# A gated linear recurrence with a gated feed-forward layer: two units transposed by DMA instead of on TensorE, float32 running sums in four units, four gate blocks in a bank, eighteen unread groups of products, and a new order of work

## The chip, the cores and the metric

The kernel runs on one core of a Trainium2 chip. The metric is the device time of one execution in microseconds. A core has five engines, each with its own in-order stream of instructions: TensorE (PE in the profile; its weight loads are PEld), VectorE (DVE), ScalarE (ACT), GpSimd (POOL) and SyncE (SP). Sixteen DMA engines move the data; here SP issues the loads, the stores and the DMA transposes, and POOL issues the weight loads and some small copies inside the core.

## The reference

Four batches of eight heads, 768 positions, head size 48. A complex decay per position and channel, its magnitude capped at 0.999, drives a linear recurrence; its real part gives the attention output, which is reshaped to 3072 rows of 384 and passed through a gated feed-forward layer of 1536 columns.

```python
mag = np.sqrt(a_re * a_re + a_im * a_im)
scale = np.minimum(mag, 0.999) / (mag + 1e-06)
a_re_n, a_im_n = (a_re * scale, a_im * scale)
for t in range(S):
    new_re = ar * S_re - ai * S_im          # ar, ai: a_re_n, a_im_n at t
    new_im = ar * S_im + ai * S_re
    kv = np.einsum('bhd,bhe->bhde', k[:, :, t], v[:, :, t])
    S_re, S_im = (new_re + kv, new_im)
    y[:, :, t] = np.einsum('bhd,bhde->bhe', q[:, :, t], S_re)
# x: y as 3072 x 384
g = x @ w_gate
gelu = 0.5 * g * (1.0 + erf(g * inv_sqrt2))
val = x @ w_val
ffn_out = gelu * val @ w_out
res_gate = 1.0 / (1.0 + np.exp(-(x @ w_res)))
return (x + res_gate * ffn_out)
```

## The kernel before

The 768 positions of a batch are cut into six chunks of 128, so there are 24 tiles (batch, chunk). They are handled in 14 units: units 0 and 1 hold the first chunk of batches 0 and 1, unit 2 the first chunk of batches 2 and 3, units 3 to 11 two tiles each (two batches of the same chunk), and units 12 and 13 the last chunk of batches 2 and 3.

A unit goes through three functions.

- `prepare` loads a_re, a_im, q, k and v of its tiles (192 KB a load, L373). ACT takes the logarithm of a_re (L394), its inverse by an exponential (L395), and, with the ratio a_im / a_re made at L397, the logarithm of the magnitude (L399, L402, L403) and the angle (L433). Both are summed along the 128 positions by a product with a triangular matrix. The summand is first split into a rounded part and a rest in the type fp32r (lh and ll, L406 and L408, for the logarithm; th and tl, L334 and L452, for the angle), and `sums` (L355, products at L359) adds two products for each tile. The capped sums are turned into exponentials (L423, L424), the angles are reduced to one turn (L462, L464) and turned into sines and cosines (L477). The last row of the angles is carried into the next chunk of the same batch by a small DMA with addition (L439, L445). From these, queries and keys with real and imaginary parts are made (L482, L487) and transposed: in units 0 to 7 on TensorE (L504, eight transposes a tile and side, followed by a copy of 96x1024 out of PSUM), from unit 8 on by a DMA transpose that SP issues (L496). `PE_T = 8` sets that.
- `attend` makes the masked products of queries and keys (L535, L538), the attention output (L547, L549) and the carried state (L559 to L572).
- `forward` transposes x (L591 on TensorE for units 0 to 2, L583 by DMA afterwards) and runs the gates and values: 12 blocks of 128 columns, two blocks to a PSUM bank, each with three products (L605). GELU on ACT (L610) and a product on DVE (L611) follow each bank. In a unit of two tiles a bank of two blocks is 512 columns wide, in a unit of one tile 256. Then come the residual gate (L620, L622), the output in three steps of four products a tile (L631), and the last two products and sums (L635, L638) before the store (L640).

Every function adds steps to a plan. The order of the 1450 steps is a list of numbers written out by hand or by a tool, `ORDER`, and the engine of many steps is written in `PLACE`. `Plan.run` walks the list; each engine gets its steps in that order, buffers and PSUM banks are handed out along it (25 wide buffers, eight banks), and a table of ACT functions is loaded (L652) whenever the next step needs another of the three sets. Some kinds of DVE and POOL steps (`PORT`) are made to wait for each other in turn. The weights come in POOL's stream (L340): six loads each for the gate and value weights (wg, wv), one for the residual weights (wr), three for the output weights (wo).

Of the kernel before, what the change touches and what calls it, by code (L numbers as in the profile page):

```python
# [9 lines left out]
FP = mybir.dt.float32  # L10
# [10 lines left out]
PE_T = 8  # L21
SL, ST = 1,1
WD = 25
# [7 lines left out]
    24: "DVE", 33: "DVE", 40: "DVE", 50: "DVE", 51: "ACT", 53: "ACT", 64: "ACT", 104: "POOL", 114: "ACT", 116: "POOL",  # L31
    132: "ACT", 145: "ACT", 190: "DVE", 191: "DVE", 203: "DVE", 213: "DVE", 223: "DVE", 225: "ACT", 236: "DVE", 252: "ACT",
    305: "DVE", 306: "DVE", 318: "DVE", 322: "ACT", 323: "POOL", 330: "DVE", 340: "DVE", 345: "DVE", 347: "ACT", 353: "DVE",
    422: "DVE", 435: "DVE", 438: "POOL", 446: "DVE", 460: "DVE", 463: "ACT", 551: "DVE", 554: "POOL", 555: "POOL", 562: "DVE",
    572: "DVE", 576: "DVE", 585: "DVE", 595: "DVE", 667: "DVE", 670: "ACT", 671: "POOL", 686: "ACT", 688: "DVE", 692: "DVE",
    771: "DVE", 786: "POOL", 787: "POOL", 821: "DVE", 866: "DVE", 872: "DVE", 899: "DVE", 902: "POOL", 903: "POOL", 910: "DVE",
    933: "DVE", 984: "DVE", 1014: "ACT", 1015: "POOL", 1050: "DVE", 1088: "DVE", 1121: "ACT", 1124: "POOL", 1125: "POOL",
    1151: "DVE", 1160: "DVE", 1198: "DVE", 1232: "POOL", 1233: "POOL", 1240: "DVE", 1251: "ACT", 1257: "DVE", 1304: "DVE",
    1325: "POOL", 1329: "DVE", 1344: "DVE", 1376: "DVE", 1396: "ACT", 1397: "POOL", 1410: "ACT", 1448: "DVE",
}  # L40
ORDER = [
    97, 98, 16, 102, 293, 17, 103, 410, 104, 21, 105, 22, 106, 294, 23, 24, 411, 179, 115, 295, 34, 35, 116, 296, 117, 107, 25,
    178, 118, 303, 26, 36, 420, 27, 37, 108, 119, 28, 100, 181, 180, 413, 304, 109, 120, 421, 110, 305, 121, 38, 29, 188, 30,
    111, 39, 306, 412, 307, 32, 99, 182, 189, 308, 112, 309, 190, 31, 125, 191, 319, 310, 101, 526, 41, 321, 122, 40, 19, 18,
    123, 320, 42, 113, 183, 299, 204, 422, 124, 205, 127, 130, 33, 527, 423, 436, 206, 43, 207, 528, 20, 529, 184, 44, 126, 314,
    192, 46, 128, 316, 193, 210, 45, 322, 208, 424, 194, 47, 195, 49, 211, 323, 131, 129, 199, 52, 196, 209, 48, 536, 315, 311,
    212, 324, 135, 425, 50, 537, 1, 185, 298, 137, 437, 54, 200, 132, 114, 138, 538, 312, 136, 198, 325, 313, 326, 426, 55, 327,
    300, 759, 297, 186, 758, 53, 7, 141, 56, 133, 197, 539, 139, 328, 643, 642, 213, 134, 201, 214, 51, 329, 60, 438, 140, 57,
    216, 439, 58, 144, 202, 2, 187, 330, 215, 334, 12, 552, 217, 8, 332, 553, 6, 0, 219, 331, 218, 226, 336, 142, 220, 768, 333,
    143, 222, 227, 145, 224, 62, 440, 761, 645, 644, 301, 302, 225, 335, 441, 223, 769, 554, 221, 242, 343, 443, 59, 555, 61,  # L50
    339, 243, 63, 240, 652, 64, 344, 444, 341, 233, 231, 442, 241, 228, 234, 317, 244, 445, 653, 146, 760, 337, 5, 342, 232,
    559, 540, 340, 874, 4, 654, 3, 245, 150, 235, 154, 560, 338, 556, 875, 561, 236, 85, 170, 360, 87, 152, 350, 156, 166, 203,
    345, 148, 361, 81, 354, 65, 171, 9, 10, 168, 446, 11, 83, 229, 162, 427, 73, 13, 164, 158, 77, 67, 75, 351, 417, 416, 160,
    557, 89, 355, 541, 79, 90, 69, 358, 74, 431, 558, 230, 71, 151, 318, 359, 770, 251, 364, 348, 365, 66, 155, 153, 349, 433,
    428, 432, 68, 362, 429, 14, 76, 363, 771, 430, 163, 655, 346, 82, 86, 70, 147, 84, 78, 347, 157, 656, 149, 249, 72, 165,
    167, 252, 159, 237, 172, 250, 884, 367, 15, 238, 357, 257, 91, 885, 88, 169, 269, 352, 80, 562, 542, 784, 447, 657, 92, 415,
    253, 239, 161, 448, 261, 543, 414, 273, 173, 366, 93, 353, 563, 564, 668, 877, 369, 174, 658, 450, 876, 434, 669, 254, 94,
    175, 368, 452, 263, 255, 449, 258, 265, 277, 259, 455, 986, 419, 418, 278, 451, 459, 267, 533, 988, 279, 256, 886, 785, 457,
    456, 275, 453, 458, 274, 280, 454, 1206, 370, 670, 435, 659, 372, 464, 374, 386, 460, 271, 671, 246, 465, 530, 382, 887,
    276, 260, 248, 1097, 388, 376, 390, 466, 461, 467, 384, 474, 476, 480, 544, 95, 1207, 392, 247, 531, 356, 475, 786, 547,  # L60
    270, 371, 468, 545, 532, 477, 548, 549, 787, 272, 469, 675, 1096, 772, 373, 262, 266, 281, 481, 987, 773, 546, 1216, 672,
    660, 534, 646, 989, 484, 535, 176, 676, 264, 268, 888, 550, 677, 478, 470, 788, 471, 479, 791, 566, 889, 663, 462, 662, 661,
    792, 96, 673, 282, 793, 287, 1106, 674, 375, 996, 568, 565, 288, 283, 463, 789, 665, 997, 485, 387, 567, 1107, 664, 647,
    473, 284, 177, 289, 391, 571, 575, 573, 377, 389, 285, 790, 900, 396, 394, 649, 648, 577, 290, 551, 678, 1098, 393, 486,
    998, 679, 572, 569, 286, 574, 680, 510, 570, 506, 487, 378, 764, 291, 576, 901, 681, 1208, 592, 650, 488, 774, 490, 511,
    397, 775, 1099, 502, 380, 492, 383, 590, 482, 683, 504, 498, 508, 591, 385, 593, 881, 651, 1306, 1209, 902, 582, 491, 999,
    395, 500, 903, 689, 379, 489, 586, 685, 381, 493, 483, 690, 1000, 594, 398, 583, 1108, 686, 776, 779, 907, 765, 595, 778,
    580, 587, 399, 581, 781, 780, 908, 1217, 596, 794, 601, 400, 904, 578, 682, 584, 472, 777, 880, 292, 1378, 684, 404, 905,
    597, 499, 1109, 579, 585, 909, 600, 1218, 687, 1311, 503, 688, 628, 691, 405, 762, 401, 763, 599, 666, 906, 1122, 696, 890,
    507, 692, 706, 795, 402, 698, 406, 505, 697, 501, 403, 693, 512, 699, 1379, 878, 1012, 589, 520, 610, 509, 1219, 796, 911,  # L70
    708, 494, 407, 1013, 618, 707, 408, 602, 709, 879, 614, 782, 598, 798, 513, 612, 629, 620, 992, 995, 1123, 604, 496, 1307,
    616, 495, 710, 700, 603, 766, 797, 891, 895, 767, 892, 619, 896, 799, 497, 1001, 521, 701, 893, 1383, 910, 716, 615, 800,
    1384, 711, 617, 1385, 1312, 894, 897, 605, 522, 783, 913, 1014, 514, 801, 611, 802, 810, 805, 898, 1313, 515, 806, 882, 717,
    1124, 523, 702, 607, 703, 621, 712, 516, 1015, 912, 1230, 613, 803, 606, 726, 804, 517, 1215, 899, 1002, 914, 993, 883, 994,
    990, 622, 1003, 608, 807, 728, 667, 588, 734, 811, 915, 808, 738, 730, 722, 991, 917, 736, 723, 916, 732, 624, 609, 814,
    623, 824, 713, 918, 740, 724, 815, 812, 822, 1314, 1016, 1004, 1213, 625, 813, 725, 825, 1220, 1006, 1019, 823, 1007, 727,
    694, 731, 524, 518, 1125, 809, 1033, 695, 1020, 1315, 729, 816, 1017, 525, 920, 919, 1021, 636, 817, 1018, 704, 1009, 1008,
    1005, 1316, 735, 1025, 519, 1102, 828, 718, 626, 637, 705, 720, 733, 737, 714, 926, 638, 1231, 1386, 832, 826, 1022, 639,
    719, 818, 630, 1026, 827, 627, 1308, 1210, 833, 1100, 927, 640, 715, 829, 1322, 721, 1129, 631, 1024, 936, 1126, 924, 937,
    641, 921, 632, 1394, 925, 1127, 739, 1232, 1130, 819, 633, 1381, 1023, 928, 1128, 929, 1028, 744, 752, 746, 934, 742, 747,  # L80
    753, 842, 1027, 1221, 1131, 1387, 1110, 741, 409, 831, 935, 1031, 1032, 1323, 1395, 844, 1309, 1030, 846, 754, 1132, 938,
    1222, 944, 939, 1317, 1111, 1112, 848, 743, 1223, 858, 834, 847, 1103, 836, 1113, 945, 745, 859, 1045, 838, 748, 930, 755,
    634, 835, 840, 1029, 1046, 849, 1324, 1114, 1047, 922, 830, 1212, 1048, 1133, 843, 1117, 1233, 1211, 1101, 635, 923, 931,
    1134, 837, 839, 1224, 950, 845, 1325, 1105, 1310, 749, 1038, 850, 1318, 1119, 1116, 1118, 841, 1319, 1115, 1136, 1104, 1320,
    1036, 1039, 946, 851, 966, 756, 1321, 1225, 1037, 1226, 1049, 757, 1135, 1380, 854, 972, 1050, 821, 852, 1214, 948, 853,
# [101 lines left out]
def kernel(  # L187
# [25 lines left out]
    if SPLIT:  # L213
        units[-SPLIT:] = [[x] for u in units[-SPLIT:] for x in u]
    NU = len(units)
    where = {bc: (p, i) for p, u in enumerate(units) for i, bc in enumerate(u)}
    size = [len(u) for u in units]

    ctx.enter_context(tc.manual_schedule())
# [463 lines left out]
```

## Time and profile before

| | us |
|---|---|
| median of the three runs shown | 262.35 |
| lowest and highest run | 261.4, 591.57 |
| the profiled execution | 262.78 |
| its span, first to last instruction | 261.0 |

The profile is one execution. It gives each engine's busy time (TensorE 226.4 us, DVE 225.4, ACT 214.1, POOL 94.5), the same by stages, the groups of instructions by line and form with the mean duration and what ended the idle time ahead of them, the waits, and a chain of work followed back from the last instruction. Of that chain TensorE has 71%, DMA 11%, ACT 9%. Over the span, HBM was read with 31.26 MB and written with 4.72 MB. "Clock" is the TensorE clock that the throttle granted, as a share of full speed; its mean was 0.978.

### The profile page before, as it was taken

To read this page: it belongs to the slowest core of one execution; us is meant where nothing else is said; L and a number is where in the kernel's file an instruction comes from. 1 tells how busy PE (TensorE), PEld (TensorE's weight loads), DVE (VectorE), ACT (ScalarE), POOL (GpSimd) and SP (SyncE) were. 2 spreads that over 40 slices of the span, in tenths; PEclk is the share of its full clock that TensorE was granted. 3 is DMA by queue.
4 is the path that set the end of the run, shared out by engine and by line. 5 is a ranking of instruction groups with operands and counts; after the bars stand their busy time and mean duration, and the time that the engine had idled before them with its cause. 6 is when DMAs were issued, how large, how long until landed. Compare 5 with 4: busy or idle time off the path is not lost.

```text
span 261.0 us, 6358 instructions
## 1 busy us (share of the span) xinstructions
PE 226.4 (87%) x2426; PEld 181.8 (70%) x2426; DVE 225.4 (86%) x404; ACT 214.1 (82%) x355; POOL 94.5 (36%) x114
## 2 busy tenths in 40 slices
PE   0230992889999999999999999999999999999993
PEld 0120772778978977877878877778778777887881
DVE  2589889999899999999999999999999794965363
ACT  4999999899899999999998999999988684241240
POOL 3013086196605743576625634351420001110110
PEclk9999996599999999999999999999999999999998
DMA  8999999989999997995989896999757919402111
GB/s 141 187 187 186 187 194 192 213 163 213 202 184 172 167 186 163 221 146 124 211 149 190 148 179 149 182 168 236 133 114 160 117 23 136 133 3 63 60 63 60
DMA packets 162174, 39.83 MB, mean 153 GB/s; under 512 B 155617, under 2 KB 162145, under 8 KB 162145
## 3 DMA queue, kind: packets, MB, share of 16 engines
q1 hardware_dynamic: 157696, 35.53, 79.4%
q0 software_dynamic: 4448, 3.90, 9.3%
q8 instruction: 19, 0.31, 0.5%
q14 instruction: 11, 0.08, 0.1%
HBM read 31.26 MB, written 4.72 MB: 138 GB/s over the span
## 4 chain that ended last, share of the span: by engine, by line
PE 71%; DMA 11%; ACT 9%; DVE 3%; POOL 2%; SPq 1%; issue 1%; POOLq 0%; DVEq 0%
PE pb L605 32%; PE pb L631 17%; PE pb L359 6%; PE pb L620 4%; PE pb L504 4%; PE pb L535 3%; DMA wo<-in_moe_w_out_dram 3%; DMA wv<-in_moe_w_val_dram 2%; DMA ai<-in_a_im_dram 2%; ACT L652 2%; DMA t<-fr 2%; DMA ar<-in_a_re_dram 2%; POOL t L397 1%; PE pb L549 1%; PE pb L547 1%; ACT CS L477 1%
## 5 line engine op out<-in xcount | busy, mean ns | idle before, releaser
L610 ACT ACTIVATE h<-pb 128x512 bf16<-128x512 f32 (+1 forms) x84 | 41.2, 547 | 23.2 <-PE pb L631 13.0
L605 PE MATMUL pb<-xT,wv 128*128 128x256 bf16 (+1 forms) x504 | 58.1, 257 | 0.4 <-DMA wv<-in_moe_w_val_dram 0.4
L605 PE MATMUL pb<-xT,wg 128*128 128x256 bf16 (+1 forms) x504 | 57.0, 257 | 0.0
L631 PE MATMUL pb<-wo,h 128*128 128x384 bf16 x288 | 56.5, 326 | 0.0
L611 DVE SCALAR_TENSOR_TENSOR h<-h,pb 128x512 bf16<-128x512 bf16 (+1 forms) x84 | 48.5, 602 | 4.2 <-PE pb L605 2.8
L605 PEld LDWEIGHTS <-wg 128*128 128x128 bf16 x504 | 42.9, 98 | 7.1 <-issue 0.8
L652 ACT ACT_TABLE_LOAD x36 | 46.2, 1283 | 1.3 <-PEq L667 0.7
L605 PEld LDWEIGHTS <-wv 128*128 128x128 bf16 x504 | 41.9, 98 | 7.5 <-issue 1.3
L638 POOL TENSOR_TENSOR ot<-ot,x 128x384 f32<-128x384 f32 x16 | 14.6, 913 | 65.0 <-DVE Gb L567 23.4
L631 PEld LDWEIGHTS <-h 128*128 128x128 bf16 x288 | 26.3, 97 | 13.0 <-issue 0.4
L538 DVE TENSOR_TENSOR am<-pb,mask 128x512 bf16<-128x512 f32 x48 | 31.9, 680 | 2.9 <-PE pb L535 2.8
L397 POOL TENSOR_TENSOR t<-t,ai 128x768 f32<-128x768 f32 (+1 forms) x10 | 16.0, 1601 | 18.1 <-DVE fK L487 9.0
L504 PE MATMUL pb<-ident,fK 128*128 128x128 bf16 x112 | 10.0, 246 | 13.5 <-DVE fK L487 13.5
L359 PE MATMUL pb<-th,ut_one 128*128 128x384 f32 x24 | 11.3, 471 | 11.4 <-POOL th L334 11.1
L452 POOL TENSOR_TENSOR tl<-t,th 128x768 fp32r<-128x768 f32 (+1 forms) x10 | 16.5, 1656 | 10.4 <-DVE ll L408 7.8
L635 DVE SCALAR_TENSOR_TENSOR ot<-sg,pb 128x384 f32<-128x384 f32 x24 | 13.1, 547 | 6.8 <-PE pb L631 5.0
L504 PEld LDWEIGHTS <-fK 128*128 128x128 bf16 x112 | 8.4, 112 | 15.0 <-DVE fK L487 14.3
L535 PE MATMUL pb<-QT,KT 96*128 96x128 bf16 x192 | 17.7, 225 | 0.5 <-DMA QT<-fQ 0.4
L535 PEld LDWEIGHTS <-KT 96*128 96x128 bf16 x192 | 13.8, 101 | 3.9 <-issue 2.2
L622 ACT ACTIVATE sg<-pb 128x384 f32<-128x384 f32 x24 | 11.6, 502 | 5.3 <-PE pb L620 2.8
L620 PE MATMUL pb<-wr,xT 128*128 128x384 bf16 x72 | 15.5, 326 | 0.0
L423 ACT ACTIVATE E<-pb 128x384 f32<-128x384 f32 x24 | 11.5, 500 | 3.2 <-PE pb L359 3.0
(91 smaller groups left out, 472.2 us busy)
## 6 DMA issues: line engine op xcount, KB each, us to landing
ar<-in_a_re_dram SPq DMA_DIRECT2D x24, 192.0 KB, 4.6
ai<-in_a_im_dram SPq DMA_DIRECT2D x24, 192.0 KB, 4.6
k<-in_k_dram SPq DMA_DIRECT2D x24, 192.0 KB, 4.4
q<-in_q_dram SPq DMA_DIRECT2D x24, 192.0 KB, 4.5
vf<-in_v_dram SPq DMA_DIRECT2D x24, 192.0 KB, 4.3
out_dram<-ot SPq DMA_DIRECT2D x24, 192.0 KB, 2.8
wg<-in_moe_w_gate_dram POOLq DMA_DIRECT2D x6, 192.0 KB, 5.6
wv<-in_moe_w_val_dram POOLq DMA_DIRECT2D x6, 192.0 KB, 5.9
```

Of the source, the lines that this page charges most:

```text
L359: nc.tensor.matmul(out=bank.tile, lhsT=ut_one, rhs=x[:, i * DM:(i + 1) * DM], start=(j == 0), stop=(j == 1))
L397: add(e1, "tai", lambda: on[e1].tensor_tensor(out=F("t"), in0=F("t"), in1=flat(T("ai"), n), op=OP.mult), [s["ai"]], [s["t"]], n)
L452: add(e10, "tl", lambda: on[e10].tensor_tensor(out=F("tl"), in0=F("t"), in1=F("th").bitcast(FP), op=OP.subtract), [s["t"], s["th"]], [s["t ...
L504: nc.tensor.transpose(out=tp.tile[:, h, :], in_=s[g].tile[:, i * H + h], identity=ident)
L535: nc.tensor.matmul(out=ap.tile[:, h, :], lhsT=kT.tile[0:DD, u * H // 2 + h, :], rhs=qT.tile[0:DD, u * H // 2 + h, :], start=True, stop=True)
L538: add("DVE", "am", lambda u=u, am=am, ap=ap: nc.vector.tensor_tensor(out=am.tile[:, u * H // 2:(u + 1) * H // 2, :], in0=ap.tile, in1=mask ...
L605: nc.tensor.matmul(out=o_.tile[:, u, :], lhsT=w_[:, k_, (2 * m + u) * 128:(2 * m + u + 1) * 128], rhs=s["xT"].tile[:, k_, 0:n].rearrange(" ...
L610: add("ACT", "gelu", lambda gp=gp, hv=hv: nc.scalar.activation(out=hv(), in_=gp.tile, func=AF.Gelu), [gp], [hh], n, "G")
L611: add("DVE", "h", lambda vp=vp, hv=hv: nc.vector.scalar_tensor_tensor(out=hv(), in0=hv(), scalar=0.5, in1=vp.tile, op0=OP.mult, op1=OP.mul ...
L620: nc.tensor.matmul(out=rp.tile, lhsT=s["xT"].tile[:, k_, i, :], rhs=wr[:, k_, :], start=(k_ == 0), stop=(k_ == KF - 1))
L631: nc.tensor.matmul(out=op_.tile, lhsT=s["h2"].tile[:, k_, i * 128:(i + 1) * 128], rhs=wo[:, k_, :], start=(k_ == 0), stop=(k_ == NF - 1))
L652: plan.run(ORDER, lambda table: nc.scalar.preload_act_table_set(ACT_SETS[table]), after)
```

## The change

The constants, and with them what is done in which unit:

```diff
-PE_T = 8
-SL, ST = 1,1
-WD = 25
+PE_T = 6
+PF_L, PF_T = 4, 4
+WD, WQ = 25, 5
+CSB = 2
+QUAD = 14
+WARM = 18
...
-PLACE = { (the old engines)
+PLACE = { (new engines for many steps)
...
-ORDER = [ (1450 steps)
+ORDER = [ (1400 steps)
```

`PE_T = 6`: units 6 and 7 are transposed by DMA too. `PF_L = PF_T = 4`: units 0 to 3 sum in float32, with one product for each sum and no split; the cap is applied in place (`cap`) and lh, ll, th and tl are not made. `QUAD = 14` leaves every unit in a group of its own, so the new functions for groups (`prepare` cut into `logs`, `angles`, `features`) work on one unit at a time, as before. a_re is loaded straight into the buffer of its logarithm.

```diff
-            if SL:
+            if p >= PF_L:
                 add("PE", "cumL", lambda i=i: sums(clm[i], i, F("lh"), F("ll")), [s["lh"], s["ll"]], [clm[i]])
             else:
...
+                add("PE", "cumL4", lambda i=i: nc.tensor.matmul(out=clm[i].make([128, DM]), lhsT=ut_f, rhs=P("la", p)[:, i],
+                                                               start=True, stop=True), [V["la"][p]], [clm[i]])
...
-        if ST:
+        if p >= PF_T:
             e9 = place("DVE")
...
+                add("PE", "cumT4", lambda i=i: nc.tensor.matmul(out=cth[i].make([128, DM]), lhsT=ut_f, rhs=P("t", p)[:, i],
+                                                               start=True, stop=True), [V["t"][p]], [cth[i]])
```

In `forward` a bank holds `w` blocks, two in a unit of two tiles and four in a unit of one:

```diff
-        for m in range(NF // 2):
+        w = 512 // (n * 128)
+        for m in range(NF // w):
...
-                    o_.make([128, 2, n * 128])
-                    for u in range(2):
+                    o_.make([128, w, n * 128])
+                    for u in range(w):
...
-            hv = lambda m=m: s["h2"].tile[:, 2 * m:2 * m + 2, 0:n * 128]
+            hv = lambda m=m: s["h2"].tile[:, w * m:w * m + w, 0:n * 128]
```

Eighteen groups of eight products of the identity with itself are added, each into a bank that nobody reads, and placed by the list:

```diff
+    for _ in range(WARM):
+        wb = Bank()
+
+        def f(wb=wb):
+            wb.make([128, 512])
+            for _ in range(8):
+                nc.tensor.matmul(out=wb.tile[:, 0:128], lhsT=ident, rhs=ident, start=True, stop=True)
+        add("PE", "warm", f, (), [wb])
```

The product that updates the carried state (`Gb`) may now be placed on POOL, and is in 11 of its 16 steps. Steps by kind, where they differ (old and new): gate and value steps 168 and 144, GELU 84 and 72, transposes of queries and keys on TensorE 28 groups and 20, by DMA 20 and 28, table loads of ACT 36 and 30. Of the 18 unread groups 14 stand ahead of the first gate step in the new list.

## The prediction

> **What bounds the kernel now.** I read the busy time by stages first, then the chain that ended last, then the groups by form, then the transfer queue's waits. The stages (length, busy time with counts, granted TensorE clock, DMA share, GB/s):
>
> ```profile
> core 0: us, PE busy (x) PEld busy (x) DVE busy (x) ACT busy (x) POOL busy (x), PEclk, DMA share, GB/s
> 0.00:55.40 55.40, 26.13 (x198) 19.85 (x198) 43.74 (x78) 49.72 (x79) 20.25 (x34) 0.91 1.26 183
> 55.40:256.70 201.30, 200.25 (x2236) 161.93 (x2231) 180.50 (x325) 164.38 (x278) 74.26 (x81) 1.00 0.81 145
> 256.70:261.00 4.30, 0.00 (x0) 0.00 (x0) 1.11 (x2) 0.00 (x0) 0.00 (x0) 0.84 0.24 91
> ...
> 45.00:51.50 6.50, 4.59 (x35) 3.90 (x36) 6.40 (x9) 5.25 (x7) 1.40 (x3) 0.50 1.21 209
> ```
>
> The first gate product starts at 55.42. Before it TensorE works 26.1 of 55.4 us while ACT works 43.4 of the 45.4 us from 10 to 55.4: ACT's queue, with DVE, sets when the gates begin. From there TensorE idles 1.05 us in 201.3, then comes a tail of 4.3. So the time is start + TensorE's work behind it + tail. The chain (start, length, what) gives the two waits behind the start, and TensorE's pace:
>
> ```profile
> 58.50 5.66 DMA wv<-in_moe_w_val_dram
> 64.21 0.51 PE pb L605 x6
> ...
> 70.11 7.25 DMA wo<-in_moe_w_out_dram
> ...
> 97.87 0.66 PE pb L605 x6
> 98.52 1.30 PE pb L631 x8
> ...
> 101.78 1.34 PE pb L504 x24
> 103.12 0.97 PE pb L620 x6
> ...
> 131.53 0.69 PE pb L359 x4
> ```
>
> A gate or value step of six products costs 0.655 us, an output step of four 0.65, a residual step 0.49, eight transposes 0.45, one running sum (a pair in fp32r) 0.345. Four query-key products cost 0.223 (0.22 to 0.23 in the same view).
>
> **The parts.** Rows used (line, form, count | busy, mean ns | idle before):
>
> ```profile
> L652 ACT ACT_TABLE_LOAD x36 | 46.2, 1283 | 1.3 <-PEq L667 0.7
> L408 DVE SCALAR_TENSOR_TENSOR ll<-la,lh 128x768 fp32r<-128x768 f32 x10 | 9.4, 949 | 0.1
> L610 ACT ACTIVATE h<-pb 128x256 bf16<-128x256 f32 x24 | 7.9, 396 | 11.8 <-PE pb L631 9.5 <-PE pb L605 2.3
> L521 PE MATMUL pb<-idf,mr 16*96 16x16 f32 x18 | 3.0, 242 | 0.0
> ```
>
> *TensorE's work behind the first gate product.* I count the steps that each list places behind it. Alike in both: gates and values 94.5 us, output 46.8, residual 11.8, query-key 8.9, the rest of attention and its small steps about 14.8; 176.8 together. The old list adds 17 transpose groups (7.7) and 34 running sums (11.5): 196.0, for which the chip took 201.3, a share of 0.973. The new list adds 10 groups (4.5), 30 sums (10.2) and 4 of the unread groups (8 x 0.056 = 0.45 each, the pace of 128-column gates at 248.13: 54 in 3.02 us), less one small step of 0.2: 193.1. At the same share: 198.4. **-2.9 us.**
>
> *The start.* ACT must run 70 instructions and 7 table loads before the old first gate, 74 and 7 before the new one: by mean durations 55.4 and 56.5 us. ACT's instructions overlap (241.7 us of durations make 214.1 busy, 0.886): **+1.0 us**. The loads needed first rise from 40 to 41, inside the same microsecond.
>
> *Float32 sums in units 0 to 3.* These drop ll, th and tl of four units (0.36 to 1.8 us each on DVE, POOL or ACT) and run 12 products in float32 in place of 12 pairs. No row shows a float32 product of 384 columns. Nearest below: the pair, 0.345. Above: the widest fp32r rows, 0.69 each early on, twice: 1.38 against a cold pair at 0.64. So 0 to +8.9 us of TensorE, in a stage where it idles 29.3. I take nothing on the end, since ACT sets the start; ends: -2.0 (ACT's idle time from 10 to 55.4, all of it) to +8.9. L521, already float32, shows 22 rows for 11 products. [...]
>
> *Unread groups.* 14 of the 18 stand ahead of the first gate, 6.3 us at full pace and 12.6 at half, where TensorE idles 29.3: nothing. What they can give: at clock 0.50 (45 to 51.5) four transpose groups came 0.87 us apart where 0.45 is the later pace, 1.7 us. I take 0, because ACT and POOL (a cast ends at 55.16, just ahead of the last attention product before the gate) are as late; ends -1.7 and 0.
>
> *Units 6 and 7 by DMA.* The eight groups are counted above; their eight copies (1.01 on ACT, 0.68 on DVE) lay beside TensorE. Added: eight issues on SP of 1.29 us, landing after 3.5, each waiting for its product tile with loads queued behind it. I take 0, as the list leaves units 8 and 9 their loads 4 us or more ahead of use; the other end is the second rival.
>
> *Four blocks a bank.* In the four single-tile units ACT goes from 24 x 0.396 to 12 x 0.607 us (-2.2), DVE from 24 x 0.414 to 12 x 0.677 (-1.8); TensorE streams the same columns. Beside TensorE: 0; in the tail the last value block's pair, 0.6 + 0.7 us, lies under three output steps and one residual step, 2.4 us.
>
> *The list.* Table loads fall from 36 to 30, 7.7 us of ACT, none ahead of the first gate. ACT idles 36.9 us behind the start, so 0; at most TensorE's last 1.05 idle goes. The weights: the last wv load moves from place 297 to 290 with its first use at 312 to 341, the last wo from 373 to 352. Their waits (0.43 and 0.28 us) stay inside the share of 0.973.
>
> **Sum.** The profiled execution took 262.78 us (span 261.0). 262.78 - 2.9 + 1.0 = 260.9; it lay 0.43 above the median of the runs, 262.35, so **260.4 us**.
>
> **Rivals.**
>
> 1. *Faster: the start comes early.* If the warm clock gives its 1.7 us, ACT loses its idle 2.0 and TensorE its 1.05: 260.4 - 4.75 = 255.7. For it: ahead of the new gate ACT has done ten roundings and sixteen exponentials of sums against seven and twelve, so less preparation is left behind it. Against: DMA is at 183 GB/s over the whole stage, and the same bytes must come. [...] Chance 0.30.
>
> 2. *Slower: SP becomes the bound.* Its waits, one of them shown (waiter, released by: us in all, times, longest):
>
> ```profile
> SPq L496 <- DVE am L538: 9.6, 3, 7.3
> ```
>
> With the other rows of L496 they add to 25.2 us for 20 transposes, 1.26 each; with the issue, 2.55. Eight more in the stretch from 84 to 142, where SP has gaps of 6.5 us in all, delay what stands behind by 20.4 - 6.5 = 13.9. The queries of unit 8 were issued by 127.5 and read at 136.2; less 4.5 for landing, 4.2 of slack. So DVE, and TensorE behind it, come 9.7 late: **270.1**. It decides once SP's added time there passes 10.7. For it: the waits are long when the list has a transpose early. Against: in that stretch many loads hold SP 1.0 to 2.4 us where 0.4 is the least, so part of the queue is DMA time that goes on during a wait. Chance 0.17.
>
> 3. *The float32 products hold the start.* One fp32r product over 384 columns took 0.32 us at half clock (starts at 34.56, 34.88, 35.20), a pair 0.64. If a float32 product takes two pairs, near the upper end above, twelve add 7.7; nine unread groups at half pace add 8.1. Together they pass the 13.2 us that TensorE idles from 10 to 40 by 2.6, at worst by all 7.7. Middle: +5.2, 265.6. For it: L521's two rows for each product. [...] Against: these products come early in each unit, when ACT has other units' work queued. Chance 0.08.
>
> That the unread products are dropped is no rival: all 144 stand in TensorE's program.
>
> **How the numbers follow.** Forecast 0.45, rivals 0.30, 0.17 and 0.08. The forecast's own range takes in -3.7 (1.7 + 2.0) and +5.2: 256.7 to 265.6. The range that should hold 8 in 10 reaches to rival 1 with the share of 0.973 gone too (-5, at 251) and to rival 2 (270). Two per cent, about what a measurement of this kernel can tell from no change, are 257.1 and 267.6. Faster: 0.27 of rival 1 and 0.04 of the forecast, 0.31. Slower: rival 2 and 0.02 of rival 3, 0.19. Within: 0.50.
>
> **What would show it.** First gate product near 56.4; span from there to TensorE's last product near 198.4; 30 table loads; transposes by TensorE 160 in place of 224. Clock under 1.00 from 40 to 51 would say the unread groups do not keep it. A float32 sum near 0.65 us or twice that, and ACT idle with TensorE as releaser before 50, would speak for rival 3; L496 waits of over 10 us from 100 to 140, with DVE waiting for q or k, for rival 2. Wrong altogether: a start before 52, or TensorE idle for more than 5 us behind it.

## The result and the profile after

The changed kernel is a little slower, where a little faster was forecast.

| | before | after |
|---|---|---|
| median of 20 runs, us | 262.18 | 263.49 |
| profiled execution, us (span) | 262.78 (261.0) | 263.42 (261.4) |
| start of the first gate product, us | 55.42 | 57.48 |
| from there to TensorE's last product, us | 201.3 | 199.9 |
| of it TensorE idle, us | 1.05 | 2.89 |
| tail, us | 4.30 | 4.04 |

Ratio after to before: 1.0057, 95% interval 1.0034 to 1.0079. The difference is below the two per cent that the prediction names, but clear of zero, and its sign is not the forecast's.

The busy time by stages of the changed kernel (length, busy time with counts, granted clock, DMA share, GB/s), to be read against the same stages of before:

```profile
core 0: us, PE busy (x) PEld busy (x) DVE busy (x) ACT busy (x) POOL busy (x), PEclk, DMA share, GB/s
0.00:57.46 57.46, 35.33 (x312) 25.56 (x313) 41.99 (x75) 51.62 (x83) 20.87 (x38) 0.91 1.20 186
57.46:257.36 199.90, 197.01 (x2201) 158.79 (x2197) 174.09 (x295) 151.94 (x257) 66.89 (x76) 1.00 0.88 154
257.36:261.40 4.04, 0.00 (x0) 0.00 (x0) 1.11 (x2) 0.00 (x0) 0.00 (x0) 1.00 0.26 97
45.00:51.50 6.50, 5.19 (x71) 4.50 (x69) 6.47 (x11) 6.16 (x10) 3.88 (x5) 0.90 1.24 192
```

Behind the start TensorE is busy 197.0 us in place of 200.25, so the saving of 3.2 us is there. It is more than given back by a start 2.06 us later and by 1.84 us more idle time. TensorE's waits from 55.4 us on (who waited for whom: us, times, longest):

```profile
PE pb L621 <- DVE am L612: 1.1, 1, 1.1
PE pb L609 <- DMA QT<-fQ: 0.8, 1, 0.8
PE pb L681 <- DMA xT<-x: 0.6, 1, 0.6
PE pb L681 <- DVE h L687: 0.5, 1, 0.5
PE pb L609 <- DVE KT L362: 0.5, 1, 0.5
PE pb L633 <- DVE fK L561: 0.4, 1, 0.4
```

The first stands just ahead of the first gate product, the others are the new idle time; the wait for QT (at 127.46) is for the second tile of unit 6, one of the two units moved to DMA transposes. The chain that ended last (start, length, what) no longer shows the weights, as it did before (wv at 58.50, wo at 70.11), but ACT, a carry by DMA and DVE until 71 us, and TensorE from there on:

```profile
53.84 0.75 ACT t L441
54.97 1.82 POOL t L444
56.81 0.84 ACT s L447
...
66.19 3.52 DMA t<-fr
69.83 0.86 DVE th L362
70.69 0.60 DVE h L687
71.33 1.50 PE pb L681 x24
```

Where the saving went shows when both kernels are compared at one moment, 85 us, a point taken behind the loads of all weights. The transfers of both kernels up to there, before first:

```profile
DMA packets 66622, 15.83 MB, mean 186 GB/s; under 512 B 63158, under 2 KB 66614, under 8 KB 66614
```

```profile
DMA packets 65561, 15.65 MB, mean 184 GB/s; under 512 B 62096, under 2 KB 65552, under 8 KB 65552
```

And the groups of TensorE behind 85 us, by form, of before and then of after:

```profile
L605 PE MATMUL pb<-xT,wv 128*128 128x256 bf16 x342 | 45.9, 273 | 0.0
L605 PE MATMUL pb<-xT,wg 128*128 128x256 bf16 x318 | 41.1, 273 | 0.0
...
L504 PE MATMUL pb<-ident,fQ 128*128 128x128 bf16 x48 | 3.7, 219 | 0.0
L504 PE MATMUL pb<-ident,fK 128*128 128x128 bf16 x48 | 3.5, 219 | 0.0
```

```profile
L681 PE MATMUL pb<-xT,wv 128*128 128x256 bf16 x360 | 46.7, 273 | 0.0
L681 PE MATMUL pb<-xT,wg 128*128 128x256 bf16 x343 | 43.5, 273 | 0.6 <-DMA xT<-x 0.6
...
L578 PE MATMUL pb<-ident,fK 128*128 128x128 bf16 x16 | 1.2, 220 | 0.0
```

Both kernels have moved nearly the same bytes by then (0.18 MB apart). The new one has 80 transposes fewer left (96 and 16; 80 x 0.056 = 4.5 us) but 43 gate and value products of 256 columns more (660 and 703; 43 x 0.109 = 4.7 us). The stages on both sides of 85 us, with the columns of the first table, two lines of before and then two of after:

```profile
55.42:85.00 29.58, 28.92 (x390) 24.38 (x387) 28.07 (x56) 27.97 (x51) 15.83 (x18) 1.00 1.18 192
85.00:256.70 171.70, 171.31 (x1849) 137.53 (x1846) 152.42 (x270) 136.38 (x228) 58.40 (x63) 1.00 0.74 137
```

```profile
57.48:85.00 27.52, 26.09 (x400) 22.64 (x396) 26.60 (x46) 26.44 (x41) 14.44 (x17) 1.00 1.13 180
85.00:257.36 172.36, 170.90 (x1803) 136.13 (x1801) 147.47 (x250) 125.48 (x217) 52.44 (x60) 1.00 0.84 150
```

Behind 85 us TensorE's work is nearly equal, 171.3 and 170.9 us. That the new kernel has more gate work left is decided ahead of 85 us: from the first gate product to there TensorE worked 28.9 us before and 26.1 after, for the start is 2.06 later and the idle time 0.8 longer, and 1.35 of the 26.1 went to three unread groups: 4.2 us less. In the same stretch the new kernel did 24 transposes more (64 against 40, 1.3 us) and six residual products fewer (1.0 us), which makes it 4.5.

### The profile page after: what moved, and what is told of

Read it like the earlier page. It is cut to its first block, busy times and chain, and to the rows that moved or that the text cites. A ratio compares the mean times of both kernels' runs of the same rounds, so it can differ in the third digit from the quotient of the medians.

```text
span 261.4 us, 6476 instructions
## 1 busy us (share of the span) xinstructions
PE 232.3 (89%) x2506; PEld 184.4 (71%) x2506; DVE 217.2 (83%) x371; ACT 203.6 (78%) x339; POOL 87.8 (34%) x113
## 4 chain that ended last, share of the span: by engine, by line
PE 63%; ACT 15%; DMA 9%; issue 4%; DVE 4%; POOL 2%; SPq 1%; DVEq 0%; POOLq 0%; ACTq 0%
PE pb L681 30%; PE pb L707 16%; PE pb L387 4%; PE pb L696 4%; PE pb L609 3%; ACT L737 3%; DMA t<-fr 2%; DMA xT<-x 2%; DMA ai<-in_a_im_dram 2%; DMA QT<-fQ 2%; POOL t L444 2%; DMA la<-in_a_re_dram 2%; ACT t L453 2%; ACT CS L463 2%; PE pb L623 1%
## 5 line engine op out<-in xcount | busy, mean ns | idle before, releaser
L686 ACT ACTIVATE h<-pb 128x512 bf16<-128x512 f32 x72 | 40.2, 604 | 22.0 <-PE pb L681 21.3
L681 PE MATMUL pb<-xT,wv 128*128 128x256 bf16 (+1 forms) x504 | 56.4, 257 | 0.5 <-DVE h L687 0.5
L687 DVE SCALAR_TENSOR_TENSOR h<-h,pb 128x512 bf16<-128x512 bf16 x72 | 47.4, 678 | 10.8 <-PE pb L681 8.8
L681 PE MATMUL pb<-xT,wg 128*128 128x256 bf16 (+1 forms) x504 | 55.1, 257 | 0.6 <-DMA xT<-x 0.6
L642 POOL TENSOR_TENSOR Gb<-U,M 96x384 bf16<-96x384 f32 x11 | 9.3, 873 | 22.1 <-DVE fK L561 11.2
L475 DVE SCALAR_TENSOR_TENSOR la<-s,la 128x768 f32<-128x768 f32 (+1 forms) x14 | 11.7, 838 | 5.8 <-ACT s L450 5.2
L529 POOL TENSOR_TENSOR tl<-t,th 128x768 fp32r<-128x768 f32 (+1 forms) x8 | 12.9, 1608 | 9.8 <-DVE fQ L561 3.3
L444 POOL TENSOR_TENSOR t<-t,ai 128x768 f32<-128x768 f32 (+1 forms) x6 | 10.1, 1677 | 18.1 <-ACT h L686 8.0
L696 PE MATMUL pb<-wr,xT 128*128 128x384 bf16 x72 | 15.1, 326 | 0.0
L542 DVE SCALAR_TENSOR_TENSOR fr<-fr,pb 128x384 f32<-128x384 int32 x24 | 12.8, 547 | 2.3 <-ACT fr L540 2.2
L725 PE MATMUL pb<-ident 128*128 128x128 bf16 x144 | 12.9, 245 | 1.5 <-POOL ident masks.py:199 1.5
```

Source lines behind the costliest of these rows:

```text
L444: add(e1, "tai", lambda p=p, e1=e1: on[e1].tensor_tensor(out=PF("t", p), in0=PF("t", p), in1=flat(st[p]["ai"].tile, size[p]), op=OP.mult), ...
L529: add(e10, "tl", lambda: on[e10].tensor_tensor(out=F("tl"), in0=PF("t", p), in1=F("th").bitcast(FP), op=OP.subtract), [V["t"][p], s["th"]] ...
L681: nc.tensor.matmul(out=o_.tile[:, u, :], lhsT=w_[:, k_, (w * m + u) * 128:(w * m + u + 1) * 128], rhs=s["xT"].tile[:, k_, 0:n].rearrange(" ...
L686: add("ACT", "gelu", lambda gp=gp, hv=hv: nc.scalar.activation(out=hv(), in_=gp.tile, func=AF.Gelu), [gp], [hh], 2, "G")
L687: add("DVE", "h", lambda vp=vp, hv=hv: nc.vector.scalar_tensor_tensor(out=hv(), in0=hv(), scalar=0.5, in1=vp.tile, op0=OP.mult, op1=OP.mul ...
L696: nc.tensor.matmul(out=rp.tile, lhsT=s["xT"].tile[:, k_, i, :], rhs=wr[:, k_, :], start=(k_ == 0), stop=(k_ == KF - 1))
```

## Experiments

All ratios are to the kernel before, on the same chip. Those whose name begins with a_ start from the changed kernel (1.0057), those with b_ from its source with the old constants and the old list. The last column is left empty where no start was read. Times worked out of ratios take the kernel before at 262.4 us.

| kernel | ratio, 95% interval | first gate, us |
|---|---|---|
| a_nowarm | 1.0088, 1.0058 to 1.0117 | |
| a_fp32r | 1.0224, 1.0189 to 1.0259 | 64.5 |
| a_pet8 | 1.0188, 1.0153 to 1.0224 | 58.2 |
| a_gb | 1.0168, 1.0125 to 1.0210 | 57.6 |
| b_ctrl | 1.0038, 1.0004 to 1.0073 | 54.9 |
| b_pet6 | 1.0278, 1.0237 to 1.0319 | |
| b_f32 | 1.0034, 1.0003 to 1.0064 | 56.1 |
| b_w4 | 1.0141, 1.0087 to 1.0196 | |
| b_allw | 1.0564, 1.0530 to 1.0598 | 56.8 |
| a_av | 1.0064, 1.0034 to 1.0095 | 55.7 |
| a_sp | 1.0297, 1.0265 to 1.0329 | 58.0 |
| a_three | 1.0300, 1.0267 to 1.0334 | 57.3 |
| a_wvav | 1.0120, 1.0045 to 1.0195 | 56.6 |
| a_pf6 | 1.0083, 1.0051 to 1.0115 | 58.2 |
| a_pf8 | 1.0063, 1.0039 to 1.0088 | 57.2 |
| a_pf6av | 1.0057, 1.0025 to 1.0088 | 56.0 |
| a_xact | 1.0130, 1.0085 to 1.0174 | 59.2 |
| a_xdma | 1.0263, 1.0232 to 1.0295 | 62.1 |

### One part taken out of the changed kernel

```diff
-WARM = 18
+WARM = 0
```

> The changed kernel without its eighteen unread groups; everything else, and the order of the other steps, stays. Theory A (the groups lie in idle time, 14 ahead of the first gate product; the 4 behind it are 1.8 us of TensorE at 0.45 each): 263.5 - 1.8 = 261.7 us, first gate product unmoved near 57.5. Rival W (they keep the clock up): the low clock of 39 to 46 us lasts longer or starts earlier, first gate 1.5 us later, time 263.3 or more. Rival H (their work itself brings the low clock on): the stage from 39 to 46 us is at full clock, first gate 1 us earlier or more, time 260.5 or less.

The middle of the ratio is 0.003 above the changed kernel's (0.8 us), and the intervals overlap. The clock is plainer: 0.935 to 0.960 in its executions, against 0.970 to 0.986 in those of the changed kernel. TensorE has 1.8 us less to do and the time does not fall. H is out. With the groups the granted clock is higher (W), but what they gain and what they cost cannot be told apart in the time.

```diff
-PF_L, PF_T = 4, 4
+PF_L, PF_T = 0, 0
```

> The changed kernel with the split sums (lh, ll, th, tl and pairs of products) back in units 0 to 3, placed in the order where the float32 ones stood. Theory A (float32 saves DVE and POOL work and costs TensorE nothing that ends late): DVE gets about 7 more instructions of 0.55 to 0.95 us ahead of the first gate, which comes 1 to 3 us later: 264.5 to 266.5. [...]

4.4 us more (0.0167 x 262.4), and the first gate 7 us later: in this list the float32 products do not hold the start, they free it.

```diff
-PE_T = 6
+PE_T = 8
```

> The changed kernel with units 6 and 7 transposed on TensorE again, at the places of the DMA transposes in the order. Theory A (the eight groups are 3.6 us of TensorE, the eight copies lie beside it, and the wait for QT of 0.8 us at 127 goes): 263.5 + 3.6 - 0.8 = 266.3. Rival Q (the DMA transposes delay the transfers behind them, and that is where the idle 2.9 us behind the start come from): 264.5 or less.

3.4 us more, near the 2.8 of theory A; Q is out. The wait for QT is gone, and one of 2.0 us for wv has come.

```diff
-PLACE: Gb on POOL in 11 of its 16 steps
+PLACE: Gb on DVE in all 16
```

> The changed kernel with all sixteen Gb products on DVE, in place of eleven on POOL. I took the move at nothing. Theory A (DVE has room behind the start; eleven of 0.55 us are 6 us, of which two stand ahead of or near the start): 263.5 within 0.7. Rival: DVE, with the waits for its h, am, KT and fK behind much of TensorE's idle time behind the start, is the tight one, and the time rises by 1.5 us or more.

2.9 us more. I had not given this part of the change a term at all. TensorE's waits from 56 us on, the longest two:

```profile
PE pb L815 <- DVE am L806: 1.8, 2, 1.1
PE pb L875 <- DVE h L881: 1.7, 2, 1.5
```

### The parts under the old list

```diff
-PE_T = 6
-PF_L, PF_T = 4, 4
-WARM = 18
-        w = 512 // (n * 128)
+PE_T = 8
+PF_L, PF_T = 0, 0
+WARM = 0
+        w = 2
-ORDER, PLACE of after
+ORDER, PLACE of before, by step
```

> The source of the changed kernel with all constants of the kernel before, its order and its engines; only a_re is loaded straight into the buffer of the logarithm. Theory A (the load's buffer matters little): 262.2 within 0.5. If the direct load is a cost by itself (the load must wait for the buffer of a logarithm that is still read): 263.5.

1.0 us above the kernel before, between the two values; the others of this group are read against it. Each of the next three takes back one line of that diff (b_pet6 PE_T, b_f32 PF_L and PF_T, b_w4 w), b_allw all of them, with the unread groups behind the TensorE steps that they follow in the new list.

> The old list and constants (as in b_ctrl), with units 6 and 7 transposed by DMA, at the places of the TensorE transposes in the old order. Undoing the part in the new list cost 266.8 - 261.4 = 5.4 us of span (medians: 3 to 5). Theory V (the part is worth as much in any list: 3.6 us of TensorE less): 263.3 - 3.6 = 259.7. Rival L (the new list is built round the part, so that undoing it there costs more than doing it gains): 261.5 to 263.3. Rival Q (the DMA transposes hold SP's queue): 265 or more.

> The old list and constants (as in b_ctrl), with float32 sums in units 0 to 3: the cap at the place of lh, ll, th and tl dropped. Undoing the part in the new list cost 268.3 - 264 = 4 us, and the first gate product came at 64.5 in place of 57.5. Theory V: DVE and POOL lose some 11 us of work ahead of the gates, so that the start of 54.9 comes 2 us or more earlier: 261 or less. Rival L: the start stays within 1 us, as ACT's order there is as full as before: 262.5 to 264. Rival F (the float32 products hold the start): 265 or more.

> The old list and constants (as in b_ctrl), with four blocks a bank in the four single-tile units, each step at the place of the second of its old pair. My step took 0: 263.3 within 0.7. Rival: ACT and DVE, shorter by 4 us in all, give 1 us at the start and in the tail: 262 or less. Rival: the first GELU of a bank comes a product group later, so that ACT and the outputs wait: 264.5 or more.

> All parts of the change (float32 sums, units 6 and 7 by DMA, four blocks a bank, the unread groups) but the old list: every step stands where its counterpart stood. Table loads as in the old list. Theory P (the parts gain by themselves and the new list gives it back): 263.3 - 3.6 - 2 = 257.7 or less, faster than both kernels. Theory L (the parts are worth little where the list is not made for them): 261 to 264, as the changed kernel. Rival: the old list can't feed the parts, DVE or SP waits: 266 or more.

Against b_ctrl: units 6 and 7 by DMA 6.3 us slower, float32 sums no change, four blocks a bank 2.7 us slower, all parts 13.8 us slower. None of the parts gains without its list. The six runs of b_w4 spread from 264.6 to 269.5 us, so its 2.7 is rough. The three parts alone add up to 9.0 of the 13.8; whether the rest comes from the unread groups or from the parts together was not tried. In b_allw TensorE stands still for the tiles of units 6 and 7 (start, length, engine, line, shapes, idle time before):

```profile
127.66 0.61 PE L803 MATMUL pb<-QT,KT 96*128 96x128 bf16 x4 [4.38 <-DMA KT<-fK]
...
156.91 0.84 PE L803 MATMUL pb<-QT,KT 96*128 96x128 bf16 x12 [2.15 <-DMA KT<-fK]
```

The two waits, 6.5 us together, are a cost of the added DMA transposes, but not on the path of the second rival: there the loads queued behind them made DVE wait for q or k, at a price of 9.7 us, and here TensorE waits for the transposed tiles themselves. In the new list 0.8 us of such a wait is left.

### TensorE's waits in the changed kernel taken away

```diff
-    ... 11, 229, 320, 88, 329, 9, 544, 513, 84, 428, ...
+    ... 11, 320, 88, 329, 9, 544, 513, 84, 229, 428, ...
```

> The changed kernel with one step moved on TensorE's queue: the attention product that waits 1.09 us for its mask just ahead of the first gate product goes behind the first two gate steps. Theory S (the start of the gates is worth its full length at the end, as my sum has it): first gate 56.2 to 56.4 in place of 57.5, and 263.5 - 1.1 = 262.4. Rival C (ACT's and DVE's preparation, busy without a gap up to 71 us, sets the pace there, not the first gate): first gate earlier by the same, but TensorE idles 1 us more between 58 and 75, and the time stays at 263.5.

The start came 1.76 us earlier and the time did not move. TensorE waits elsewhere before 85 us:

```profile
62.06 0.37 PE L827 MATMUL pb<-v,fK 128*128 128x48 bf16 x8 [1.80 <-DVE fK L755]
...
65.21 0.73 PE L875 MATMUL pb<-xT,wv 128*128 128x128 bf16 x10 [0.92 <-DMA wv<-in_moe_w_val_dram]
...
77.77 1.46 PE L901 MATMUL pb<-wo,h 128*128 128x384 bf16 x8 [0.47 <-DMA wo<-in_moe_w_out_dram]
...
81.35 1.46 PE L901 MATMUL pb<-wo,h 128*128 128x384 bf16 x8 [0.78 <-DMA wo<-in_moe_w_out_dram]
```

By that start 10.01 MB had landed. So the start is no term of a sum by itself: something else paces the first 85 us.

```diff
-    ... 577, 1072, 269, 568, 1073, 1192, ...  670, ...  669, 863, ...
+    ... 577, 269, 568, 1192, ...  670, ...  669, 1072, 1073, 863, ...
-    ... 984, 965, 614, ...  919, 812, ...
+    ... 984, 614, ...  919, 965, 812, ...
```

> The changed kernel with three loads moved on SP's queue: two a_im loads of unit 10 behind the DMA transposes of unit 6's second tile, one query load of unit 9 behind the transpose of x of unit 8. Theory S (the 0.8 and 0.6 us that TensorE waited for QT at 127 and xT at 174 are lost at the end): both waits go, 263.5 - 1.4 = 262.1. Rival D (the transposes take their time in the DMA engines, which are over 100% busy there, so that moving them on the queue gives little): the waits stay above 0.5 us each, 263.2 or more.

A miss by 8 us: 6.3 slower. Both waits went, but the a_im loads of unit 10, two transposes later on SP's queue, held DVE at the product that reads them, and TensorE behind DVE. This is the path of the second rival, made by the order of SP's queue. DVE's longest wait from 100 to 160 us, and TensorE's from 56 on:

```profile
DVE t L638 <- DMA ai<-in_a_im_dram: 6.1, 1, 6.1
```

```profile
PE pb L875 <- DVE h L881: 6.1, 1, 6.1
```

> The changed kernel with both moves (the attention product behind two gate steps; three loads on SP's queue) and one cast of v (0.81 us) taken from ACT to POOL ahead of the start. Theory S: 1.1 + 1.4 us from the moves, and 0.8 from ACT: 260.2 to 261.0, faster than the kernel before by some 0.6%. Rival C: only the 1.4 of the loads, or less: 262 to 263.5.

The same stall (5.8 us) covers the rest of that kernel, so its time tells nothing of the cast on POOL. The first gate product, at 57.3, came 1.6 us later than in a_av (55.7).

> The changed kernel with the earlier start of a_av, and the four loads of wv that POOL issued at 57.3 put ahead of its product of unit 6 (issued at 55): Rival W (the start of a_av was lost to the weights): no wait for wv, 262.4. Theory D (DVE): the wait for fK at 62 stays near 1.8 us, others come in the place of wv's: 263.5 or more.

No wait for wv is left, but TensorE waits 3.4 us for fK at 64.8. The interval is wide (runs from 264.1 to 270.6); it is not faster. Weights moved ahead in the stream put something else behind.

### Less work on DVE

```diff
-PF_L, PF_T = 4, 4
+PF_L, PF_T = 6, 6
```

> The changed kernel with float32 sums in units 4 and 5 as well: no lh, ll, th, tl there, eight pairs of products become eight float32 products. Theory D (DVE and ACT pace the stretch from 43 to 85 us): two ll of 0.95 on DVE, one tl on DVE, one on POOL, one th on ACT (0.83) and one on POOL go: 1 to 3 us earlier, 260.5 to 262.5. Rival F (TensorE's float32 products are what is late there): 263.5 or more. Rival W (the weights' loads): 263.5, the waits as they are.

> The same with float32 sums in units 4 to 7. Theory D: units 6 and 7 have their sums between 70 and 100 us, where DVE is 93 to 99% busy: another 0.5 to 1.5 us, 259.5 to 262. Rival F: eight more float32 products of 0.4 to 0.65 us for pairs of 0.345 fall where TensorE has no idle time: 264 or more.

> Float32 sums in units 0 to 5 and the attention product behind the first two gate steps (the earlier start that by itself gave nothing). Theory D: with less on DVE the earlier start pays, 0.5 to 1.5 us below a_pf6: 259.5 to 261.5. Rival W: TensorE waits for wv (near 65) and wo (near 77 to 82) instead, no faster than a_pf6.

None differs from the changed kernel. DVE's busy time from 43 to 85 us falls from 41.0 to 38.9 and 37.5 us, and TensorE waits for wv instead (1.4 us in both). Theory D, formed after a_gb, falls: more on DVE costs, less gives nothing.

### One suspected cost added to

```diff
+        add("ACT", "extra", lambda: nc.scalar.activation(out=wo[:, 0:2, :]..., in_=mask.to_broadcast([128, 6, 128]), func=AF.Identity, scale=1.0))
```

> The changed kernel with four more instructions of 128x768 on ACT, their results unread, spread over its queue between about 14 and 45 us: 4 x 0.74 = 3.0 us by the pace of such instructions in the rows of ACT. Theory A (ACT's queue paces the kernel up to the gates, and what is late there is late at the end): first gate at 60.5 in place of 57.5, 266.5. Rival M (the loads pace it, ACT would only wait for them less): first gate at 58.5 or earlier, 264.5 or less.

The four took 0.83 us each, 3.3 in all. The start moved by 1.7 us, the time by 1.9 (0.0073 x 262.4): between the two theories.

```diff
+        add("SP", "extra", lambda z=z: nc.sync.dma_start(out=wo[:, 2 * z:2 * z + 2, :]..., in_=q[z, :, 640:768, :]...))
```

> The changed kernel with four more loads of 192 KB, unread, spread over SP's queue between about 8 and 30 us: 0.79 MB, 4.2 us at the 186 GB/s that the loads run at there. Theory A (ACT): part of it hidden, first gate at 59 or earlier, 264 to 265.5. Rival M (the loads pace it): first gate near 61.7, and 267 or more.

The first gate products of the two kernels:

```profile
59.21 1.50 PE L876 MATMUL pb<-xT,wg 128*128 128x128 bf16 x24
```

```profile
62.11 1.50 PE L876 MATMUL pb<-xT,wg 128*128 128x128 bf16 x24
```

4.2 us of loads, issued between 17 and 41 us, moved the start by 4.6 us and the time by 5.4 (0.0206 x 262.4): all of it, and more. The stage from 10 us to the first gate product, in the changed kernel, in a_xact and in a_xdma:

```profile
10.00:57.48 47.48, 33.46 (x297) 23.96 (x298) 39.85 (x67) 45.41 (x74) 19.65 (x27) 0.89 1.23 192
```

```profile
10.00:59.21 49.21, 33.27 (x296) 23.65 (x297) 39.74 (x67) 48.49 (x80) 19.86 (x27) 0.90 1.23 192
```

```profile
10.00:62.11 52.11, 33.51 (x296) 23.53 (x297) 40.00 (x67) 45.73 (x75) 19.85 (x27) 0.90 1.15 190
```

ACT, the fourth busy time of each line, is idle 2.07 us in the changed kernel, 0.72 in a_xact and 6.38 in a_xdma. The added loads made ACT wait 4.3 us more, nearly all that the start moved by. The added ACT work, 3.08 us of busy time here, used up 1.35 of ACT's idle time, and the rest is what the start moved by. So the loads pace this stage, with ACT close behind them. Whether it is the transfers' rate or also the four places on SP's queue was not separated.

## Why the prediction was wrong

**TensorE's work: right.** Forecast -2.9 us; its busy time behind the start fell by 3.2.

**The start: the first step that failed.** The prediction read ACT's queue as what sets the start, and took +1.0 us by mean durations and a factor of 0.886. The start moved by 2.06. ACT's busy time ahead of it rose by 1.90 (49.72 to 51.62), so even as an ACT term it was half the size. The path was wrong too, in two ways. Just ahead of the gates TensorE waits 1.09 us for the mask of one attention product; with that product behind the first two gate steps (a_av) the start came at 55.7, and the time did not move. And in what comes before that, ACT follows the loads (a_xdma), with 2 us of idle time of its own (a_xact). That DMA ran at 183 GB/s over the whole stage I named only as an argument against a faster start. By the first gate 10.16 MB had landed before and 10.68 MB after, but this is no cause of the later start: a later start lets more land, and a_av began its gates with 10.01 MB.

**The form of the sum: failed with it.** Start + work + tail takes a saving anywhere behind the start as a saving at the end. a_av shows that start and idle time trade against each other up to 85 us, and the two kernels have nearly the same bytes moved and the same work left there.

**The share of 0.973: the largest miss.** I kept it from before. It held 1.05 us of idle time; the new list has 2.89, in waits for QT, xT, h, KT and fK of 0.4 to 0.8 us each. What each of them is worth at the end stays open: a_sp took those for QT and xT away and put a longer one in their place.

**The zeros.** The parts that I put at nothing came out so:

- Float32 sums: zero alone (b_f32), worth 4.4 us in the new list (a_fp32r). A float32 product took two rows in the changed kernel, which began 0.64 us apart from 12.6 to 15.1 us and 0.32 apart from 26.1 to 27.1 and from 32.4 to 33.1: 1.28 and 0.64 a product, where my bounds were 1.38 and the pair's 0.345. The granted clock was 1.00 in these stretches, and 1.00 too from 34 to 36 us of the kernel before, where I read a pair at half clock. So half clock is not shown there, and no run shows what makes the early products slower. The third rival's cost was there, its consequence wasn't, as the first 57 us are not TensorE's.
- Unread groups: I took 0 between -1.7 and 0. The clock rose as the lower end had it (0.970 to 0.986 with them, 0.935 to 0.960 without); on the time they give some -0.8, with intervals that overlap.
- Units 6 and 7 by DMA: 6.3 us slower under the old list (b_pet6), where TensorE waits for the transposed tiles (6.5 us in b_allw); 0.8 us of such a wait is left in the new one. SP's waits ahead of the transposes stayed below 3 us each (the longest 2.7).
- Four blocks a bank: slower alone, by a rough 2.7 us; not tried alone in the new list.
- Gb on POOL had no term, and is worth 2.9 us in the new list.
- Loading a_re straight into the buffer of its logarithm had no term either. With it and the old list (b_ctrl) the kernel was 1.0 us slower, interval 0.1 to 1.9.

**Signs.** 30 table loads, as said. The first gate product was to come near 56.4 (57.48), the span behind it was to be 198.4 (199.9). Clock under 1.00 from 40 to 51 us came (0.90 from 45 to 51.5, 0.50 before), so the groups do not keep it there alone.

**The sum again.** Forecast 260.9 for the profiled execution, measured 263.42: the start 1.1 us, idle time and work behind it 1.5 (1.8 more idle, 0.3 less work), the time around the span 0.2, the tail -0.3. The 0.43 us taken off for the median was right for before (0.60 against twenty runs) and wrong for after (-0.07). The time lies inside the forecast's own range, 256.7 to 265.6, by luck: the upper end stood for float32 products that hold the start, and they do not.

**What stays open.** Of the parts taken out of the new list, float32 sums, the DMA transposes and Gb on POOL cost time when they go, and the unread groups make no clear difference; every part put under the old list costs or gives nothing. So each list seems fitted to its own parts, which is argued and not shown, and a part's worth apart from any list was not found. Why the old list gets 4.7 us more of gate work done from the same bytes by 85 us is accounted for nearly (4.5) by start, idle time, unread groups and the transposes done there, but no run isolated the steps that cause it. No kernel here beat the one before.

## What to carry to other kernels

Where loads pace the first part of a kernel, count a saving of the busiest engine at the end only if the work left behind that part really shrinks: compare bytes moved and work left at one common moment. Carry no idle time over from an old order to a new one. Taking away a wait tells little if the next is as near. Adding a known amount of work to each suspected resource told in one run each how much slack loads and ACT have; read the idle time of the other engine along with the time. In a kernel whose order is a fitted list, taking a part out measures the part and the misfit together.

## What the runs showed of the hardware

In a_sp TensorE stopped at 125.98 us and went on at 132.09. The granted clock was 1.00 up to 128 us, 0.74 from 128 to 129, 0.50 from 129 to 135 and 0.85 from 135 to 136. In a_three, around a stall of 5.8 us, TensorE worked 0.15 us of 125 to 126, 0.06 of 130 to 131 and nothing between; the clock was 1.00 up to 129, 0.71 from 129 to 130, 0.50 from 130 to 136 and 0.88 from 136 to 137. In b_allw four output products took 0.81 us ahead of the stall of 4.4 us (at 122.47) and 1.49 behind it (at 130.19 and at 132.43). a_sp, around its stall of 6.1 us (length, TensorE's busy time, clock, DMA share, GB/s):

```profile
120.00:126.00 6.00, 5.98 (x49) 1.00 0.93 123
126.00:132.00 6.00, 0.00 (x0) 0.71 0.95 187
132.00:135.00 3.00, 2.91 (x14) 0.50 1.33 180
135.00:140.00 5.00, 5.00 (x50) 0.97 0.93 190
```

The six gate products just behind the stall, at 132.09, took 1.44 us, where six took 0.82 ahead of it, at 124.28. The changed kernel's clock is 1.00 in all four of these stretches. Its span is 7.4 us shorter (261.4 in place of 268.8), 6.1 of it the stall itself; the 14 products at clock 0.50 cost some 1.5 us by an estimate, half of their 2.91, but smaller waits differ too, so the remaining 1.3 cannot be put to the clock alone.
